# An order of its own for each down stage of a fused mLSTM + GELU kernel

## The chip, the cores and the metric

The kernel runs on one core of one Trainium2 chip. The metric is device microseconds of one execution. The engines are TensorE (PE, with its weight loads shown apart as PEld), VectorE (DVE), ScalarE (ACT), GpSimd (POOL) and SyncE (SP, whose queue issues nearly all DMAs). Each engine works through its own instructions in the order in which the kernel writes them.

## The reference

An mLSTM cell over 4 batches, 8 heads, 768 time steps and head size 40, and a two-layer network with exact GELU (320 to 2048 to 320) on its 3072 output rows. All is float32.

```python
for t in range(S):
    m_new = np.maximum(f_gate[:, :, t] + m, i_gate[:, :, t])
    f_stab = np.exp(f_gate[:, :, t] + m - m_new); i_stab = np.exp(i_gate[:, :, t] - m_new); m = m_new
    C = f_stab[:, :, None, None] * C + i_stab[:, :, None, None] * np.einsum('bhd,bhe->bhde', vt, kt)
    n = f_stab[:, :, None] * n + i_stab[:, :, None] * kt
    denom = np.maximum(np.abs(np.einsum('bhd,bhd->bh', n, qt)[:, :, None]), 1.0)
    y[:, :, t] = 1 / (1 + np.exp(-o_gate[:, :, t])) * np.einsum('bhde,bhe->bhd', C, qt) / denom
x = y.transpose(0, 2, 1, 3).reshape(B * S, H * D)
h = x @ w_in
out = (0.5 * h * (1.0 + erf(h / sqrt(2)))) @ w_out
```

## The kernel before

The sequence is cut into six chunks of 128 steps (c = 0 to 5). Within a chunk the cell is computed as an attention block (scores, weighted by exps of the gates) plus a part from the state carried over from earlier chunks. A chunk's 512 rows then go through the network: an *up* stage (x @ w_in, GELU into the tile `g`) and a *down* stage (g @ w_out). While chunk c is in its down stage, the cell of chunk c+1 is computed in the gaps, so that its rows are ready for the next up stage.

The first chunk and the second's cell follow the order FRONT; the last chunk has a code of its own. Each of the four down stages between (c = 1 to 4, the second to the fifth chunk) follows the order DOWN, a string of steps which `play` carries out one after the other. A word is a letter and, for a step of the cell, the batch (0 to 3). Since every engine keeps the order of the program, the string sets each engine's queue. The letters, with the engine and line of their work:

| word | step | work |
|---|---|---|
| M | mask | POOL L449, on the tile W of gate sums; batch 3's lies in a part of `g` |
| W | weights | ACT L475, 8 exps, in place in W |
| G | gate | ACT L481, sigmoid of the output gate, in `ob` |
| K, Q | transposes of k and q | DVE L497 into kT, qT (two buffers each); Q2 also issues POOL's `vw` (L534) |
| D3 | `vw` of batch 3 | POOL L534 |
| L3 | load of batch 3's k and q | POOL two memsets L487, SP four loads L171 |
| B3 | load of batch 3's gate sums into `g` | SP L188 |
| S0, S2 | scores of two batches | PE L563 (64x64 tiles), DVE L569: times W, four multiplies for each batch |
| C0, C2 | reads of the state, two batches | PE L618 into two banks pf |
| h0, h2 | state update, two batches | PE L629 into the same banks; POOL L642 state times decay; DVE L638 far and L644 state add |
| V | values | PE L665 (128x32 tiles), DVE L673 add; V0 also issues loads of k and v of batch 3 (SP L153) |
| Y | finish | ACT L680 Abs into `den` (one buffer), POOL L681 max and L682 multiply, DVE L686, L687; for batch 0 then ACT L694, a copy to `y_rest` |
| X | transpose of y | PE L705 into px (two banks), ACT L694 copy to `y_rest` for the next batch, L715 x_hi |
| R | split of x | DVE L728 x_lo, L729 x_all; frees px |
| F | half a product, 8 matmuls | PE L1073 |
| N | late sums | DVE L1099, two operations on `g`; what they write is read by F11 and F12 |
| Z | part of a weight sum, in the second chunk only | DVE L783 |
| j | loads for the next cell | SP L171 and L163, up to 20 DMAs |

The down product is made of seven products over halves (a Strassen-like scheme), each in two halves: F1 to F14, one for each F in the string. F1, F2, F5 and F6 accumulate in one PSUM bank, F3 and F4 in a second, F7, F8, F11 and F12 in a third, F9, F10, F13 and F14 in a fourth; two banks stand for the four, and a new one takes the bank that came free first: F7 that of F3 and F4, F9 that of F1 to F6. What follows a product on another engine is written directly behind it:

```python
todo = ((A(0, 0), Bm[0][0], 0, True, p1), (Sm(g.s2), T[2], 1, True, p6),
        (A(1, 0), Bm[1][0], 0, False, p2), (Sm(g.s1), T[1], 2, True, p5),
        (A(0, 1), T[3], 3, True, p7), (A(1, 0), Bm[1][1], 2, False, p3),
        (A(1, 1), T[4], 3, False, p4))
```

p1 (behind F2, L1088) and p2 (behind F6, L1094) are copies on ACT; p6, p5, p7, p3 and p4 (behind F4, F8, F10, F12 and F14, L1084) are adds on DVE, the last two with the sends of the output. F5 has to wait for p1, since it adds into the bank that p1 reads; F11 for p5, F13 for p7.

Exp, Sigmoid and Gelu lie in different function tables of ACT; each change shows as an ACT_TABLE_LOAD.

Of the kernel before, what the change touches and what calls it, by code (L numbers as in the profile page):

```python
# [25 lines left out]


FRONT = """
    I2 O0 g0 L0 P0 L1 E k1 t0 P1 P2 w0 k7 N k2 w1 O1 K L2 Q s0 O3 w2 q D
    k2 d P3 t1 w3 c0 L3 J v0 t2 K K y0 s1 I7 v1 I8 O2 J g1 L4 I5 c1 K I1  # L30
    I2 y1 s2 x0 t3 B4 O4 B5 g2 J x1 s3 v2 c2 L5 y2 H T0 x2 G0 v3 g3 c3 K y3
    M1 J L6 J A x3 M0 K W0 O7 K A O6 O5 J M2 W1 S0 C0 K J J T1 U U
    K L7 V0 K T2 r J J A G2 K G1 Y0 W2 S1 K M3 C1 A J S2 J K W3 K
    V1 C2 Y1 T3 J J U U S3 V2 K K J G3 J Y2 C3 X0 K V3 J K F J F
    K K B8 F J K F F J K F F F R0 X1 J J K F J F K X2 F J
    K F J Y3 K F R1 e J F Z B9 B10 F X3 R2 Z R3 F p"""
DOWN = """
    M0 F Z F L3 W0 M1 Z W1 S0 C0 F F h0 Q2 F K2 G1 D3 B3 Z V0 G2 M2 W2 M3 W3 V1 K3 Q3 F G0 S2 Z Y0 G3 C2 h2 F
    F Y1 X0 V2 V3 F N F j R0 Y2 Y3 X1 F F X2 R1 F R2 X3 R3 F"""


@with_exitstack
def kernel(
# [18 lines left out]
    B, H, S, D = q.shape  # L62
    L = P
    NCH = S // L
# [79 lines left out]
    def load(n, first=0, end=4):  # L144

        if n >= NCH * B:
            return
        c, b = divmod(n, B)
        for src, dst in ((q, qb), (k, kb), (v, vb), (o_gate, None))[first:end]:
            if dst and swapped(c, b):  # L150
                x, to = src[b, :, c * L:(c + 1) * L, :].rearrange("h p d -> p h d"), dst[turn_of(n)][:, :, 0:D]
                for i in range(2):
                    nc.sync.dma_start(out=to[halves[i]], in_=x[halves[1 - i]])  # L153
                continue
            nc.sync.dma_start(out=dst[turn_of(n)][:, :, 0:D] if dst else out_of(n),  # L155
                              in_=src[b, :, c * L:(c + 1) * L, :].rearrange("h p d -> p h d"))
# [136 lines left out]
    def decays_turned(e0, e1, g0, g1):  # L293
        e, g = slice(e0, e1), slice(g0, g1)
        gates_turned((ew[:, e], ewT[:, e]), (gg[:, g], gT[:, g]))

    def decays_last(g0, g1):
        g = slice(g0, g1)
        pd = ps_tr.tile([P, g1 - g0, BH], F32, name="pd", tag="tr")
        nc.tensor.matmul(pd.rearrange("p c n -> p (c n)"), last, gT[:, g].rearrange("p c n -> p (c n)"),  # L300
                         start=True, stop=True)
        by_half = pd.rearrange("p c (n two) -> p c n two", two=2)
        for hip in range(2):
            nc.vector.tensor_copy(out=dec[halves[hip], g], in_=by_half[halves[hip], :, :, hip])
# [65 lines left out]
    def conv_one(i):  # L370

        if i < len(pieces):
            n = bits[i].shape[1]
            lo, hi = bits[i][:, :, 0], bits[i][:, :, 1]
            s = sig[i] = raw.tile([P, WP], F32, name="sig", tag="sig")[:, 0:n]
            p = pow2[i] = raw.tile([P, WP], F32, name="pow", tag="pow")[:, 0:n]
            su, pu = s.bitcast(U32), p.bitcast(U32)

            nc.vector.tensor_scalar(out=pu, in0=hi, scalar1=20, scalar2=0x7FF,  # L379
                                    op0=OP.logical_shift_right, op1=OP.bitwise_and)  # L380
            nc.scalar.activation(out=p, in_=pu, func=AF.Relu, scale=-I23, bias=e_hi)  # L381
            nc.scalar.activation(out=pu, in_=p, func=AF.Relu, scale=-1.0, bias=e_lo)

            nc.vector.tensor_scalar(out=su, in0=hi, scalar1=0xFFFFF, scalar2=0x100000,
                                    op0=OP.bitwise_and, op1=OP.bitwise_or)
            nc.vector.scalar_tensor_tensor(out=s, in0=lo, scalar=2.0 ** -32, in1=su, op0=OP.mult, op1=OP.add)

    def conv_two(i):

        if i < len(pieces):  # L390
            hi, p = bits.pop(i)[:, :, 1], pow2.pop(i)
            pu = p.bitcast(U32)
            nc.vector.scalar_tensor_tensor(out=pu, in0=hi, scalar=0x80000000, in1=pu,
                                           op0=OP.bitwise_and, op1=OP.bitwise_or)
            dst, s = pieces[i][1], sig.pop(i)
            nc.vector.scalar_tensor_tensor(out=dst, in0=s, scalar=2.0 ** -20, in1=p, op0=OP.mult, op1=OP.mult)  # L396
            fetch(i + NB)
# [430 lines left out]
    def first_up_steps(h):  # L828

        def step(k):  # L830
            ups.append((len(ups) + len(tags_next) % 2, (2 * k, 2 * k + 2, HT * h, HT * h + HT)))
            if len(ups) == 2:
                first_up()

        return [lambda k=k: step(k) for k in range(HF // 2)]

    def first_up():
        if len(ups) == 1:
            tags_next.append(1)
        if ups:  # L840
            up_step(first_g, ups)
        ups.clear()
# [201 lines left out]
    def first_down_steps(g):  # L1044
        po = []

        def row(f):

            if f == 0:
                po.extend(ps_mm.tile([P, DM], F32, name="po", tag="ab"[b // 2]) for b in range(B))  # L1050
            for b in range(B):
                nc.tensor.matmul(po[b], g.t[:, f, b * L:(b + 1) * L], w_out[:, f, :], start=(f == 0),  # L1052
                                 stop=(f == NF - 1))
                if f == NF - 1:
                    if b % 2 == 0:
                        o_sb = outp.tile([P, 2, DM], F32, name="o_sb", tag="o_sb")
                    nc.scalar.copy(out=o_sb[:, b % 2, :], in_=po[b])
                    send(0, b, o_sb[:, b % 2, :])

        return [lambda f=f: row(f) for f in range(NF)]  # L1060
# [64 lines left out]
    def play(order, steps):  # L1125

        for word in order.split():
            if word[0] not in "AU":
                first_up()
            steps[word[0]](*[int(x) for x in word[1:].split(",") if x])  # L1130

    def in_turn(steps):
        todo = list(steps)
        return lambda: todo.pop(0)() if todo else None

    def cell_steps(c, letters, before=None):
        cell = Cell(c)
        cell.before = before
        return dict(zip(letters, (cell.mask, cell.weights, cell.gate, cell.turn, cell.scores, cell.carry, cell.values,
                                  cell.finish, cell.turn_y, cell.split_x, cell.load_last, cell.turn_k,  # L1140
                                  cell.turn_q, cell.weigh_last, cell.read_two,
                                  cell.last_M, cell.scores_two, cell.load_next, cell.update_two)))

    def first_blocks():

        copy_chunk(2, range(1))
        for r in (32, 96):
# [5 lines left out]
    steps = dict(P=fetch, L=lambda n: load(n, 0, 2), O=lambda n: load(n, 2, 4), B=load_M, E=second_gates, N=later_gates,  # L1153
                 I=keep_clock, k=warm, D=lambda: decays_turned(0, 2, 0, 1), Q=lambda: decays_turned(2, NCH - 1, 1, NCH - 1),
                 d=lambda: decays_last(0, 1), q=lambda: decays_last(1, NCH - 1), r=halves_out, p=halves_back,
                 A=in_turn(first_up_steps(0)), U=in_turn(first_up_steps(1)), e=first_blocks, F=in_turn(first_down_steps(first_g)),
                 K=in_turn(lambda i=i: conv_one(i) for i in n_pieces), H=products_begin,
                 J=in_turn(lambda i=i: conv_two(i) for i in n_pieces), Z=split_weight)
    steps |= cell_steps(0, "mwgtscvyx") | cell_steps(1, "MWGTSCVYXR")
    play(FRONT, steps)  # L1160
    for c in range(1, NCH):
        if c + 1 == NCH:
            down = LastDown()
            up(None, [], [], down)
            down.products()
            break
        g, later = Hidden(True), []
        steps = cell_steps(c + 1, "MWGTscVYXRLKQDCBSjh", g)
        up(g, weight_sum(1) + weight_sum(2) + weight_sum(3) if c == 1 else [], [lambda b=b: (steps["K"](b), steps["Q"](b)) for b in range(2)])
        if c == 1:  # L1170
            later = weight_sum(4)
        products, late = down_steps(c, g)
        steps |= dict(F=in_turn(products), Z=in_turn(later), N=late)
        play(DOWN, steps)


# [28 lines left out]
```

## Time and profile before

| | us |
|---|---|
| time, median of 3 runs (lowest, highest) | 463.55 (462.91, 463.84) |
| profiled execution, its own time | 463.01 |
| its span, first to last instruction | 461.1 |
| up stages of c = 1 to 4, each | 26.49 |
| down stage of c = 1: 154.99 to 198.70 | 43.71 |
| down stage of c = 2: 225.19 to 268.38 | 43.19 |
| down stage of c = 3: 294.87 to 337.58 | 42.71 |
| down stage of c = 4: 364.07 to 404.82 | 40.75 |
| up and down of c = 5: 404.82 to 461.10 | 56.28 |

Stages are cut where the chain of waits passes from up to down products. In a timeline a row is a group of like instructions with its start, its length, the count, and in brackets the idle time of the engine before it with what ended that. The fifth chunk's down stage (c = 4) is shorter because the last cell updates no state: h0 and h2 have no matmuls there.

### The profile page before, as it was taken

What the parts mean: (1) busy time and instruction counts of PE and PEld (TensorE: products, weight loads), DVE (VectorE), ACT (ScalarE), POOL (GpSimd) and SP (SyncE); (2) the same over time, 40 slices, a digit from 0 to 9 for tenths busy, and PEclk for the clock granted to TensorE, in tenths of its full rate; (3) what the DMA queues carried; (4) which work ended last, traced back from release to release, by engine and by line L of the source; (5) the groups of instructions that cost most, each with busy time, mean ns of one, the idle gap of its engine ahead of it and who ended that gap; (6) DMA issues with size and microseconds to landing.
All of it is one profiled execution on the core that took longest, in us unless ns stands there. A gap on an engine that the chain in (4) does not pass through costs nothing.

```text
span 461.1 us, 13165 instructions
## 1 busy us (share of the span) xinstructions
PE 453.0 (98%) x5432; PEld 402.1 (87%) x5432; DVE 337.8 (73%) x740; ACT 247.3 (54%) x541; POOL 77.9 (17%) x117
## 2 busy tenths in 40 slices
PE   8999999999999999999999999999999999999996
PEld 8787888877788898998899998899998899988996
DVE  8899879798868988754578754578654577699950
ACT  6986999854454594113494113395113395157701
POOL 3002020000010342300542200542300422100000
PEclk9999999999999999999999999999999999999999
DMA  8997993258967655219955219953018950210001
GB/s 153 206 216 190 211 221 97 73 131 226 157 164 157 117 91 97 66 50 181 161 88 95 66 58 179 156 93 46 4 57 170 166 99 13 80 36 2 1 0 58
DMA packets 174876, 51.12 MB, mean 111 GB/s; under 512 B 154752, under 2 KB 168352, under 8 KB 174816
## 3 DMA queue, kind: packets, MB, share of 16 engines
q1 hardware_dynamic: 174496, 49.95, 53.4%
q8 instruction: 43, 0.70, 0.7%
q10 hardware_dynamic: 320, 0.33, 0.2%
q14 instruction: 17, 0.14, 0.1%
HBM read 45.47 MB, written 10.03 MB: 120 GB/s over the span
## 4 chain that ended last, share of the span: by engine, by line
PE 93%; DVE 3%; DMA 2%; SPq 1%; issue 1%; ACT 0%; DVEq 0%
PE po L1073 26%; PE pu L957 23%; PE po L1052 8%; PE pu L814 6%; PE pu L968 6%; PE po L927 6%; PE ph L665 4%; PE ps L563 3%; PE pu L820 2%; PE px L705 2%; PE pf L618 2%; PE ps L547 1%; SPq L155 1%; PE pf L629 1%; PE cold L228 1%; DMA ob<-in_o_gate_dram 1%
## 5 line engine op out<-in xcount | busy, mean ns | idle before, releaser
L1073 PE MATMUL po<-w_out,g 128*128 128x160 f32 x512 | 74.4, 302 | 0.0
L972 ACT ACTIVATE g<-pu 128x512 f32<-128x512 f32 x64 | 32.2, 620 | 77.4 <-PE pu L968 77.4
L1073 PEld LDWEIGHTS po<-w_out,g 128*128 128x128 f32 x512 | 70.1, 190 | 1.9 <-ACT g L972 1.3
L957 PE MATMUL pu<-x_hi,w_in_hi 128*128 128x512 f32 x160 | 39.0, 387 | 0.0
L475 ACT ACTIVATE W<-W,aT 128x128 f32<-128x128 f32 x128 | 38.7, 388 | 0.1
L957 PE MATMUL pu<-x_lo,w_in_lo 128*128 128x512 f32 x160 | 37.8, 379 | 0.0
L449 POOL TENSOR_SCALAR_AFFINE_SELECT W<-W 128x1024 f32<-128x1024 f32 (+2 forms) x20 | 24.1, 1209 | 80.3 <-DMA W<-M_d 70.0
L1073 PE MATMUL po<-w_sums,sums 128*128 128x160 f32 x256 | 36.9, 302 | 0.0
L1073 PEld LDWEIGHTS po<-w_sums,sums 128*128 128x128 f32 x256 | 35.0, 190 | 0.4
L1052 PE MATMUL po<-w_out,g 128*128 128x320 f32 x128 | 35.2, 433 | 0.0
L957 PEld LDWEIGHTS pu<-x_hi,w_in_hi 128*128 128x128 f32 x160 | 29.5, 189 | 5.7 <-ACT g L972 1.3
L957 PEld LDWEIGHTS pu<-x_lo,w_in_lo 128*128 128x128 f32 x160 | 30.2, 189 | 4.3
L1052 PEld LDWEIGHTS po<-w_out,g 128*128 128x128 f32 x128 | 24.0, 190 | 9.6
L534 POOL TENSOR_TENSOR vw<-vb,ewT 128x328 f32<-128x328 f32 x12 | 8.8, 745 | 136.3 <-DMA vb<-in_v_dram 90.7
L569 DVE TENSOR_TENSOR W<-ps,W 128x256 f32<-128x256 f32 (+1 forms) x48 | 18.1, 416 | 17.0 <-PE ps L563 7.1
L957 PE MATMUL pu<-x_all,w_mid 128*128 128x512 f32 x80 | 30.3, 379 | 0.0
L957 PE MATMUL pu<-x_all,w_in_mid 128*128 128x512 f32 x80 | 30.3, 379 | 0.0
L814 PE MATMUL pu<-first_x,w_in 128*128 128x256 f32 x128 | 29.0, 382 | 0.0
L814 PEld LDWEIGHTS pu<-first_x,w_in 128*128 128x128 f32 x128 | 23.8, 190 | 3.4 <-DVE w_in L396 0.3
L801 DVE TENSOR_TENSOR sums<-g 128x512 f32<-128x512 f32 x16 | 12.3, 770 | 19.6 <-ACT g L972 19.6
L773 DVE TENSOR_TENSOR w_in_mid<-w_in_hi,w_in_lo 128x512 fp32r<-128x512 f32 x20 | 13.7, 685 | 16.5 <-PE pu L957 16.5
L381 ACT ACTIVATE pow<-pow,e_hi 128x320 f32<-128x320 uint32 (+1 forms) x26 | 16.1, 620 | 15.2 <-DVE pow L379 15.2
(199 smaller groups left out, 952.1 us busy)
## 6 DMA issues: line engine op xcount, KB each, us to landing
W<-M_d SPq DMA_DIRECT2D x16, 512.0 KB, 5.3
bits<-in_moe_w_in_dram SPq DMA_DIRECT2D x20, 256.0 KB, 4.3
bits<-in_moe_w_out_dram SPq DMA_DIRECT2D x16, 320.0 KB, 3.2
blocks<-kq_d SPq DMA_DIRECT2D x32, 128.0 KB, 3.2
ob<-in_o_gate_dram SPq DMA_DIRECT2D x24, 160.0 KB, 4.5
out_dram<-o_sb SPq DMA_DIRECT2D x36, 80.0 KB, 2.0
kq_d<-in_k_dram SPq DMA_DIRECT2D x32, 80.0 KB, 2.5
kq_d<-in_q_dram SPq DMA_DIRECT2D x32, 80.0 KB, 2.4
```

The source lines that it names most:

```text
L381: nc.scalar.activation(out=p, in_=pu, func=AF.Relu, scale=-I23, bias=e_hi)
L449: nc.gpsimd.affine_select(out=x, in_=x, compare_op=OP.is_ge, fill=1.0e30, base=base, pattern=[[0, H], [1, x.shape[2]]], channel_multiplier=-1)
L475: nc.scalar.activation(out=W[n][:, h, :], in_=src, func=AF.Exp, scale=-1.0, bias=aT[:, self.c, r:r + 1])
L569: nc.vector.tensor_tensor(out=w[r, :, t], in0=ps[i][hip][r, :, t], in1=w[r, :, t], op=OP.mult)
L665: nc.tensor.matmul(ph[r, h, :], Pm[:, h, r], vb[turn_of(n)][:, h, :], start=True, stop=True)
L814: nc.tensor.matmul(banks[-1][e][:, i - i0, :], in_tile(i, x)[:, e, i % 2 * P:(i % 2 + 1) * P], first_x[:, x, t0:t1], start=(x == 0 and i = ...
L927: nc.tensor.matmul(in_pairs(po[t]), x[:, t * L:(t + 1) * L], in_turns(w), start=(f, k) == first, stop=(f, k) == last, skip_group_check=True)
L957: nc.tensor.matmul(in_pairs(pus[i][e]), w[k][:, e, i * P:(i + 1) * P], in_turns(x[:, k, :]), start=(n == 0 and k == 0), stop=False, skip_g ...
L968: nc.tensor.matmul(in_pairs(pu[e]), w[r, i // 2, i % 2 * P:(i % 2 + 1) * P], in_turns(x[r, NX, :]), start=False, stop=(n == 2), skip_group ...
L972: nc.scalar.activation(out=g.t[:, HF * e + i, :], in_=pu[e], func=AF.Gelu, scale=4097.0)
L1052: nc.tensor.matmul(po[b], g.t[:, f, b * L:(b + 1) * L], w_out[:, f, :], start=(f == 0), stop=(f == NF - 1))
L1073: nc.tensor.matmul(bank[k][:, t, :], lhs(j, t), rhs(j), start=(first and t == 0 and j == 0), stop=(t == 1 and j == HF - 1), skip_group_che ...
```

## The change

DOWN is replaced by three orders: DOWN1 for c = 1, DOWN2 for c = 2 and 3, DOWN3 for c = 4. They have the words of DOWN in another order. FRONT is only broken into lines differently.

```diff
-DOWN = """
-    M0 F Z F L3 W0 M1 Z W1 S0 C0 F F h0 Q2 F K2 G1 D3 B3 Z V0 G2 M2 W2 M3 W3 V1 K3 Q3 F G0 S2 Z Y0 G3 C2 h2 F
-    F Y1 X0 V2 V3 F N F j R0 Y2 Y3 X1 F F X2 R1 F R2 X3 R3 F"""
+DOWN1 = """
+    M0 F W0 G1 K2 M1 W1 M2 L3 G2 Q2 F B3 S0 C0 h0 Z K3 D3 F F G0 V0 F Q3 V1 W2 M3 W3 j F Y0 F Y1 S2 C2 G3 h2 F
+    X0 R0 F V2 N Z V3 Y2 Z X1 Z Y3 F F X2 R1 F R2 F X3 R3 F"""
+DOWN2 = """
+    M0 K2 M1 W0 W1 G1 F S0 C0 h0 M2 G2 Q2 G0 F F L3 B3 K3 D3 Z Q3 F M3 V0 V1 Y0 W2 j F F W3 S2 C2 Z h2 F Y1 F
+    F X0 N Z G3 V2 V3 R0 F Y2 Y3 F Z X1 F X2 R1 R2 F X3 F R3"""
+DOWN3 = """
+    G1 F M0 M1 W0 W1 K2 S0 C0 h0 M2 D3 G2 F F F Q2 B3 L3 M3 V0 K3 G0 V1 F W2 j F Q3 W3 S2 Z C2 h2 Y0 Z Y1 F F
+    X0 F N G3 V2 V3 F R0 Y2 Z X1 Y3 F F Z X2 R1 R2 F X3 F R3"""
...
-        play(DOWN, steps)
+        play(DOWN1 if c == 1 else DOWN2 if c < NCH - 2 else DOWN3, steps)
```

In all three, the first state update (h0) stands directly behind S0 and C0; DOWN has F3 and F4 between. L3 stands behind M1 and M2 (in DOWN ahead of both), K2 ahead of S0. The exps and sigmoids run W0 W1 G1 G2 W2 W3 G0 G3 in DOWN, W0 G1 W1 G2 G0 W2 W3 G3 in DOWN1, W0 W1 G1 G2 G0 W2 W3 G3 in DOWN2 and G1 W0 W1 G2 G0 W2 W3 G3 in DOWN3. In DOWN2 Y0 stands ahead of W2, in DOWN1 Y0 and Y1 ahead of S2, and in DOWN2 and DOWN3 R3 stands behind F14.

## The prediction

> **What bounds the kernel now.** I read the page first, then busy time by stage, then the chain of waits and the timeline of each down stage. The page:
>
> ```profile
> PE 453.0 (98%) x5432; PEld 402.1 (87%) x5432; DVE 337.8 (73%) x740; ACT 247.3 (54%) x541; POOL 77.9 (17%) x117
> PE 93%; DVE 3%; DMA 2%; SPq 1%; issue 1%; ACT 0%; DVEq 0%
> ```
>
> TensorE is the bound nearly everywhere, so an order can gain only what PE loses between its instructions. Busy time in the four down stages (window, its length, PE, PEld, DVE, ACT, POOL):
>
> ```profile
> 154.99:198.70 43.71, 42.87 (x813) 41.27 (x814) 35.74 (x84) 23.78 (x60) 15.90 (x22) 1.00 0.47 88
> 225.19:268.38 43.19, 42.88 (x814) 41.30 (x814) 31.67 (x68) 23.78 (x60) 15.02 (x22) 1.00 0.50 91
> 294.87:337.58 42.71, 42.66 (x814) 41.17 (x814) 30.70 (x68) 23.79 (x60) 16.29 (x21) 1.00 0.37 58
> 364.07:404.82 40.75, 40.65 (x751) 39.57 (x750) 29.46 (x60) 24.15 (x61) 12.67 (x15) 1.00 0.37 70
> ```
>
> Idle PE is 0.84 in the second chunk, 0.31 in the third, 0.05 and 0.10 in the last two. The second chunk's loss is at S2, where the timeline of PE shows
>
> ```profile
> 174.39 1.44 PE L563 MATMUL ps<-qT,kT 64*64 64x128 f32 x56 [0.55 <-DVE qT L497]
> 177.38 0.73 PE L629 MATMUL pf<-vw,kb 128*40 128x41 f32 x27 [0.29 <-issue]
> ```
>
> DVE is late with K3 and Q3. The chain of waits shows the same in the third chunk, and its absence in the fifth, as the length of S2; and what a product costs behind other work:
>
> ```profile
> 243.78 1.72 PE ps L563 x44
> ...
> 381.72 1.50 PE ps L563 x64
> ...
> 390.60 4.54 PE po L1073 x32
> 395.14 0.33 PE px L705 x3
> 395.47 4.35 PE po L1073 x32
> ```
>
> A pair of products behind a V (128x32 tiles) takes 4.54, behind an X (128x128) 4.35: each return from small tiles costs 0.19. ACT in the second chunk's stage, where every change between Exp and Sigmoid has a table load:
>
> ```profile
> 159.62 0.43 ACT L1088 COPY o_sb<-po 128x320 f32<-128x320 f32 x1 [2.51 <-issue]
> 160.06 1.28 ACT L475 ACT_TABLE_LOAD   x1
> 161.36 4.78 ACT L475 ACTIVATE W<-W,aT 128x128 f32<-128x128 f32 x16
> 166.15 1.28 ACT L481 ACT_TABLE_LOAD   x1
> 167.45 0.83 ACT L481 ACTIVATE ob<-ob 128x320 f32<-128x320 f32 x2
> ```
>
> **The change, by stage.** FRONT has the same words. Each new order has the same 61 words as DOWN, so nothing is added but table loads. Below, t runs from the stage's first product; durations are the rows' (W 2.45, G 0.47, S 1.50, C 0.92, h 0.74, V 0.75, X 0.33, F 2.18).
>
> *Second chunk, DOWN1.* ACT ends the gelus at t=2.2. The order W0 G1 W1 G2 F2 .. G0 W2 W3 .. F6 needs five loads ahead of F6's copy, DOWN's W0 W1 G1 G2 W2 W3 three. F2's copy is done at 2.2 + 4 loads 5.2 + two W 4.9 + two G 0.9 + 0.4 = 13.6; F6's at 13.6 + G0 0.5 + load 1.3 + W2, W3 4.9 + 0.4 = 20.7 (19.8 before). PE, h0 now behind C0: F1, F2 4.54, S0 1.50, C0 0.92, h0 0.74, F3, F4 4.54, V0 0.77 gives 13.0 when F5 comes, which adds into the bank that F2's copy still reads: it waits 0.65. S2 comes at 21.4, when K3 and Q3 (DVE, 18.2) are done: the 0.84 is gone. The tail is worse. Y0 and Y1 now stand before S2's multiplies on DVE, and Y0's Abs (ACT) behind W3 and F6's copy, at 20.9. A Y is Abs 0.20, POOL 0.23 and 0.81, DVE 0.49 in a row with gaps, about 1.9, and Y1 waits for `den` (one buffer): they end at 22.6 and 24.8, and DVE, done with V1's add at 18.7, has nothing else meanwhile. DOWN starts those multiplies at 21.2 (176.07). From 24.8 DVE has no gap: S2's multiplies 3.1, h2 2.3, F8's add 0.5, R0 1.0, V2's add 0.5, N 2.85, Z 0.5, V3's add 0.5, Y2 0.75 gives 36.7, and ACT's copy to y_rest 37.05; PE, from S2 at 21.4 by the rows of S2, C2, h2, F8, X0, F9, V2, V3, X1, F10 and F11, is at X2 at 35.9 and waits 1.1. Then Z, Z 1.05, Y3 1.7 and F10's add 0.45 give 39.95; F13 adds into the bank which that add reads. F13, X3 and F14 end at 39.95+2.18+0.33+2.18 = 44.7: **+1.0**.
>
> *Third and fourth, DOWN2.* ACT keeps the grouping (W0 W1 G1 G2 G0, then W2 W3, G3: four loads as before), and M1 no longer stands behind L3's memsets on POOL, so W0 starts at 2.2 and not behind F2's copy. h0 behind C0 makes four groups of small tiles instead of five, 0.19 each stage; S2 (at 18.2) finds Q3 done at 14.7, 0.22 each. PE alone would end at 41.9 from the rows, and DOWN's own rows add up to 42.48 where the fourth chunk measures 42.71, so 42.1 is the floor. But Y0 stands before W2, and its copy to y_rest (ACT) ends with a chain: L3's two memsets (0.94 each) now stand on POOL behind the two state multiplies, M2 and vw and end at 9.5; three of L3's four loads and B3 wait behind them on SP, as do V0's kb and vb (landing near 16 and 18, wanted at 20.7 and 29: hidden); B3 issues at 10.3 and lands 4.6 later (the page's median for g<-M_d), M3 1.8 to 17.0, then Y0's max, multiply and DVE's share to 18.6, copy 18.9. W2: load and exps to 22.65; F6's copy 0.4; W3 to 25.5. DVE: S2's multiplies end 27.15, h2 29.4, Y1 30.15, add 30.6, N 33.4, adds 34.3, R0 35.3, add 35.75, Y2 36.55, Y3 38.55, add 39.0, R1 40.0. F11 meets N's halves within 0.1. X2 waits 0.1 for y_rest (37.1), X3 0.4 for R1, which frees its bank; X3 and F14 end at 42.55. That is **-0.65** for the third and **-0.15** for the fourth. R3 now stands behind F14's add (0.49): the next up stage wants x_lo 1.73 (8 matmuls of 0.216) after F14 and has it after about 1.2; without that cover 0.5 each.
>
> *Fifth, DOWN3.* One more load (G1 first), but F2's copy is done at 12.2 for F5 at 13.0, S2 meets Q3 with 1.1 to spare, X3 meets R1 with 0.6. No state is updated, so DOWN has four groups already. **0**, bounds -0.1 to +0.5.
>
> j's 20 loads and copies issue as soon as Q2 frees `blocks`, as now (172.44), and only sends stand behind them. The state update behind its reads frees nothing else: its POOL half waits only for C0's reads already.
>
> What no row shows is a bank or DVE handing over in these orders; I bound the second chunk by F5's wait alone (+0.65-0.84 = -0.2) and by the late copy shifting the whole tail (+2.0), third and fourth by the floor (-1.1, -0.6) and by +1.1 each. I take the walked values, whose links are nearly all rows of this trace. Sum: 1.0-0.65-0.15+0 = +0.2 on an execution of 463.01 (span 461.1, 1.9 around it), 0.54 below the median of 463.55; so 463.8.
>
> On the loads the Trainium skill speaks against the change ("ScalarE: Activation LUTs", What ACT_TABLE_LOAD costs): about 2.66 for a switch, of which 1.38 is a drain. The trace disagrees: the load at 160.06 lasts 1.28 and the exps start at 161.36. By the page F2's copy would come 5.5 later and F6's 6.9, and an estimate of the sum from its figure is +7.1 instead of +0.2.
>
> **The rivals.**
> 1. *Only PE's savings come*, the tails being hidden: the second chunk loses its 0.84, third and fourth reach 42.1 (-1.1, -0.6): 463.55-2.5 = 461.0, or 462.3 if half of it comes. For: PE is 98% busy and ACT 54%. Against: F5 and the DVE tail above are sums of rows. 0.18.
> 2. *Y0's copy holds up W2 in DOWN2.* R1 at 40.0 already stands 0.4 behind PE, so from M3's end at 17.0 on every further us is one at the stage's end. For: in the fifth chunk M3 came 5.15 after B3's issue (371.45 to 376.60), not 4.6, and loads of `blocks` took up to 6.0 where 3.4 is the median. Against: half of the delay would overlap. At 1.1 in each of two stages: 463.8+2.2 = 466.0. 0.30.
> 3. *Single activations between two loads don't hide the switch*, as the rows of 16 and 8 exps may: each of the five switches ahead of F6's copy then costs as much as two loads, 1.28 more, and the second chunk 6.4 more than the forecast: 470.2. Against: at 166.15 and 168.28 only two sigmoids stand between loads, and nothing is idle. 0.02. The page named above has this rule.
> 4. *The order does nothing*, since K2 still waits for S0's reads of kT (two buffers) and DVE takes the rest as before: 463.55. Against: M1, W0 and h0 do move. Within the forecast.
>
> **How the numbers follow.** A measurement of this kernel tells about 0.2% (0.93) from no change. The forecast, second chunk paying what the third and fourth win, has 0.50, with its own range 462.7 to 464.9; it is mostly "same", with 0.02 below and 0.06 above. Rival 1 gives faster 0.18, rival 2 and 3 slower 0.32. Faster 0.20, same 0.42, slower 0.38. The range takes in more than half of rival 1 (to 462.0; 0.07 is below) and two thirds of rival 2 (to 466.8, where the two stages lose 1.5 each; 0.10 of it and rival 3 are above).
>
> **What would show it.** The second chunk's stage at 44.7, ACT with six table loads ahead of its last gelu load, F5 idle some 0.6 behind ACT's copy at L1088, X2 behind y_rest; PE never waiting for qT. The third's and fourth's both near 42.5, idle before X3 for DVE's x_all, POOL's M3 ahead of Y0. Fifth unchanged. I am wrong if the second chunk's falls below 43.7, if the middle ones stay above 43.2, or if an up stage leaves 26.49.

## The result and the profile after

| | before | after |
|---|---|---|
| time, median | 463.52 us (6 runs) | 465.53 us (6 runs) |
| profiled execution, and its span | 463.01, 461.1 | 464.30, 462.3 |
| down stage c = 1 | 43.71 | 44.44 |
| c = 2 | 43.19 | 42.62 |
| c = 3 | 42.71 | 42.94 |
| c = 4 | 40.75 | 41.40 |

The ratio of the times is 1.0041, 95% interval 1.0027 to 1.0055: the changed kernel is slower by 0.4%. The profiled execution of after was the fastest of its six: by the medians the change costs 2.0 us, and its profile shows 1.2 of them. The four stages together lose 1.04 of the 1.2 us by which the spans differ. The up stages measure 26.49 or 26.50 as before.

Busy time of each engine over the span, and the chain that ended last by engine, from the page of after:

```profile
PE 451.2 (98%) x5432; PEld 400.3 (87%) x5432; DVE 332.9 (72%) x740; ACT 252.0 (55%) x544; POOL 74.4 (16%) x117
PE 73%; DVE 9%; ACT 7%; DMA 4%; SPq 3%; issue 2%; POOL 2%; DVEq 0%; ACTq 0%; POOLq 0%
```

TensorE is busy for 1.8 us *less* than before and the execution is longer all the same. Of the 1.8, 1.1 lie in the first 10 us (PE busy for 7.61 instead of 8.70), ahead of every changed stage, and 0.69 in the four stages. There the orders do remove work between small tiles, and more than that comes back as idle time of PE. The chain's share of other engines rises from 7% to 27%. By stage (window, length, busy PE, PEld, DVE, ACT, POOL):

```profile
155.06:199.50 44.44, 42.91 (x813) 40.88 (x814) 34.05 (x84) 26.59 (x62) 13.22 (x19) 1.00 0.46 87
225.99:268.61 42.62, 42.40 (x815) 41.07 (x814) 28.83 (x66) 23.89 (x60) 13.13 (x20) 1.00 0.50 88
295.10:338.04 42.94, 42.33 (x814) 40.96 (x814) 28.43 (x66) 23.89 (x60) 12.46 (x19) 1.00 0.35 56
364.53:405.93 41.40, 40.73 (x749) 39.62 (x750) 25.72 (x58) 25.67 (x62) 7.57 (x12) 1.00 0.34 66
```

PE busy is 0.48 and 0.33 less in the two middle stages and 0.08 more in the fifth chunk's; PE idle is 1.53, 0.22, 0.61 and 0.67 where it was 0.84, 0.31, 0.05 and 0.10. The timeline of PE names each gap (start, length, group, and in brackets the idle time before it):

```profile
168.61 2.44 PE L1076 MATMUL po<-w_out,g 128*128 128x160 f32 x16 [0.57 <-ACT o_sb L1091]
191.23 0.41 PE L708 MATMUL px<-ident,ob 128*128 128x128 f32 x2 [0.44 <-DVE ob L690]
194.56 2.44 PE L1076 MATMUL po<-t,g 128*128 128x160 f32 x16 [0.52 <-DVE o_sb L1087]
...
265.92 0.41 PE L708 MATMUL px<-ident,ob 128*128 128x128 f32 x2 [0.17 <-DVE x_all L732]
...
316.44 0.19 PE L621 MATMUL pf<-state,qT 64*64 64x41 f32 x1 [0.55 <-issue]
...
378.23 0.27 PE L668 MATMUL ph<-vb,W 128*32 128x41 f32 x3 [0.61 <-issue]
```

The first three are F5 behind ScalarE's copy of p1, X2 behind a Y, and F13 behind p7's add, all in the second chunk. The fourth is X3 behind R1. The last two are of another kind: the last matmul of C2, and the last three of the 128 of V0 and V1, start late with nothing that they wait for; "issue" means that the profile shows no cause. V1's inputs were long there: DVE's last multiply for it ended at 376.10. These two gaps are what the prediction has no step for.

### The profile page after: what moved, and what is told of

It is laid out like the page before. It is cut to its first block, busy times and chain, and to the rows that moved or that the text cites. A ratio compares the mean times of both kernels' runs of the same rounds, so it can differ in the third digit from the quotient of the medians.

```text
span 462.3 us, 13146 instructions
## 1 busy us (share of the span) xinstructions
PE 451.2 (98%) x5432; PEld 400.3 (87%) x5432; DVE 332.9 (72%) x740; ACT 252.0 (55%) x544; POOL 74.4 (16%) x117
## 4 chain that ended last, share of the span: by engine, by line
PE 73%; DVE 9%; ACT 7%; DMA 4%; SPq 3%; issue 2%; POOL 2%; DVEq 0%; ACTq 0%; POOLq 0%
PE pu L960 23%; PE po L1076 14%; PE po L1055 7%; PE pu L817 6%; PE po L930 6%; PE pu L971 5%; DMA blocks<-kq_d 3%; PE ph L668 3%; ACT W L478 2%; PE pu L823 2%; SPq L174 1%; PE ps L550 1%; PE px L708 1%; PE ps L566 1%; SPq L158 1%
## 5 line engine op out<-in xcount | busy, mean ns | idle before, releaser
L452 POOL TENSOR_SCALAR_AFFINE_SELECT W<-W 128x1024 f32<-128x1024 f32 (+2 forms) x20 | 21.3, 1073 | 82.5 <-DMA W<-M_d 61.6
L697 ACT COPY y_rest<-ob 128x128 f32<-128x128 f32 x16 | 4.7, 296 | 41.7 <-DVE ob L690 35.3
L804 DVE TENSOR_TENSOR sums<-g 128x512 f32<-128x512 f32 x16 | 11.0, 688 | 18.7 <-ACT g L975 18.7
```

The lines of the kernel that those rows point to most:

```text
L452: nc.gpsimd.affine_select(out=x, in_=x, compare_op=OP.is_ge, fill=1.0e30, base=base, pattern=[[0, H], [1, x.shape[2]]], channel_multiplier=-1)
```

## The experiments

Two theories. **A**: TensorE ran out of program. **B**: it waits for data or a buffer that the profile does not name. What A rests on: the page lists the queue that brings programs,

```profile
q8 instruction: 42, 0.69, 0.7%
```

that is pieces of 16 KB each, nearly all TensorE's (5432 weight loads and 5432 matmuls are 42.4 times 256). The trace has the times of these reads. One read ran from 375.70 to 376.93, and the DMA view of 375.6 to 377.0 shows it beside 1435 small packets of the kernel's own loads:

```profile
q1 hardware_dynamic: 1435, 0.12, 75.0%
q8 instruction: 1, 0.02, 5.5%
```

1.30 us after its end V1 went on. Counting all TensorE instructions that the trace records (weight loads, matmuls, semaphore waits), every gap named issue stands within one instruction of place 192 of 256: a border between pieces. The Trainium skill ("Runtime: NRT & Kernel Launch", Instruction fetch mechanics) states that the program comes in blocks of 256 instructions and the next is fetched while the current one runs. It calls the cost of crossing mostly hidden; that is where it and these traces part.

The table gives all kernels that ran. Stages run here from the record of the first down matmul to that of the first up matmul, 0.2 shorter than above; "issue" is the sum of PE's gaps of that name over 0.14 us from c = 1's down stage to c = 4's. Ratios are to the kernel before on the same chip.

| kernel | time | ratio (interval) | c=1 | c=2 | c=3 | c=4 | issue |
|---|---|---|---|---|---|---|---|
| before | 463.23 to 463.69 | 1 | 43.51 | 42.99 | 42.51 | 40.55 | 0.55 |
| after | 465.53 | 1.0041 (1.0027, 1.0055) | 44.24 | 42.42 | 42.73 | 41.20 | 1.16 |
| again (the change) | 465.35 | 1.0036 (1.0023, 1.0048) | 44.22 | 43.08 | 42.35 | 41.49 | 0.88 |
| only1 | 464.66 | 1.0021 (1.0010, 1.0031) | 44.23 | 43.60 | 42.80 | 40.44 | 0.84 |
| only2 | 463.55 | 1.0000 (0.9988, 1.0012) | 43.11 | 42.58 | 44.09 | 40.45 | 1.71 |
| only3 | 464.61 | 1.0015 (1.0006, 1.0023) | 43.66 | 42.73 | 43.10 | 41.34 | 0.62 |
| shift12 | 463.53 | 1.0006 (0.9997, 1.0016) | 44.23 | 42.12 | 43.03 | 40.41 | 0.50 |
| shift44 | 466.78 | 1.0062 (1.0048, 1.0077) | 44.24 | 44.53 | 42.68 | 40.34 | 2.46 |
| bshift40 | 465.10 | 1.0041 (1.0024, 1.0057) | 42.99 | 44.27 | 42.51 | 40.45 | 1.43 |
| bshift76 | 465.82 | 1.0051 (1.0034, 1.0068) | 44.20 | 42.71 | 43.25 | 41.86 | 2.73 |
| group | 463.93 | 1.0009 (0.9996, 1.0023) | 42.73 | 42.88 | 42.87 | 41.73 | 1.77 |
| f5first | 464.56 | 1.0024 (1.0013, 1.0035) | 44.22 | 42.44 | 43.27 | 41.12 | 1.10 |
| only1g | 462.95 | 0.9986 (0.9976, 0.9996) | 42.73 | 43.23 | 43.17 | 40.48 | 0.77 |
| best8 | 462.32 | 0.9977 (0.9965, 0.9988) | 42.64 | 43.23 | 42.81 | 40.33 | 0.50 |

### One order at a time: only1, only2, only3, again

```diff
+        play(DOWN1 if c == 1 else DOWN, steps)          # only1
+        play(DOWN2 if c in (2, 3) else DOWN, steps)     # only2
+        play(DOWN3 if c == 4 else DOWN, steps)          # only3
```

only1: 

> DOWN1 in the second chunk alone, DOWN in the other three. Theory A (the walk by queues): the second chunk's down stage is 44.4 us as in the profile of the change (43.7 before), the others as before; the kernel loses about 0.7 us, ratio 1.0015. Theory B (PE runs dry of instructions: the 0.55 and 0.61 us gaps named issue in the fourth and fifth chunk come from the denser small-tile work): no such gap above 0.3 us outside the second chunk, and the loss is again 0.7. Theory C (the part of the 2.0 us loss that the profiled execution doesn't show, 1.2 us, belongs to the second chunk): the loss is near 2 us.

only2: 

> DOWN2 in the third and fourth chunk alone. Theory A: the third chunk's stage 42.6 (43.2 before), the fourth's 42.4 without a gap named issue (42.7 before): the kernel gains 0.5 to 0.9 us, ratio 0.998 to 0.999. Theory B: the gaps come with the denser small-tile groups, 0.3 to 0.6 us in each stage: the fourth's is 42.9, and the kernel gains 0.3 or nothing. Theory C2 (the unseen 1.2 us belongs to DOWN2, by loads that land late in front of K2, K3 or M3): the kernel loses 0.5 us or more.

only3: 

> DOWN3 in the fifth chunk alone. Theory A: no change (40.75), ratio 1.000. Theory B: one gap named issue of 0.6 us in this stage, as in the change: a loss of 0.6 us, ratio 1.0014. Theory C3 (the unseen 1.2 us belongs here): a loss of 1.5 us or more.

again: 

> The change as it is, on the same chip, for a second profile of it. Theory A: the three parts add up to it, within 0.5 us; the stages are again 44.4, 42.6, 42.4 to 42.9 and 40.8 to 41.4. Theory B: gaps named issue again, 0.5 us or more in all over the before, at the same instructions. Theory C: a stage that is over 0.5 us longer than in the first profile holds the unseen 1.2 us.

The parts add up: +0.21%, 0.00% and +0.15% are 0.36%, again measures 0.36%. By time, then, the loss comes with DOWN1 and DOWN3, each known to some 0.1%. But a part is more than its own stage, since an order also moves what stands behind it: of only1's 0.97 us the second chunk's stage holds 0.72, and the third, still in DOWN, has a gap named issue of 0.84 in V3 where before has 0.26, which no theory for only1 allowed. DOWN1's 44.2 with its three waits is the same in each profile that has it with G1 in its old place. DOWN2 gained nothing by time (expected 0.5 to 0.9 by A, 0.3 or nothing by B). It brings its gain and loses it elsewhere: 42.58 in the third chunk, and 44.09 in the fourth, with the largest gap of all, at the same place as in after. From only2's timeline of PE:

```profile
317.08 0.25 PE L625 MATMUL pf<-state,qT 64*64 64x41 f32 x2 [1.71 <-issue]
```

DOWN3's stage is 0.65, 0.79 and 0.94 longer than before's in after, only3 and again, in the first and the last by the gap in V1 (0.61, 0.88). In only3 the border lies 3 matmuls earlier and the read of the next piece begins at 374.24 instead of 375.70; V1 runs through, so the 0.6 us that B expected came without B's gap: a second weakness takes the place: K3's load lands late, and S2 takes 2.25 instead of 1.39. From only3's timeline of DVE:

```profile
381.47 0.71 DVE L504 STREAM_TRANSPOSE kT<-blocks 128x512 f32<-128x512 f32 x1 [2.78 <-DMA blocks<-kq_d]
```

again has two stages outside what was expected of it. The fifth, with its gap of 0.88, is one; the third, 43.08, is 0.66 longer than after's, with no gap named issue. By its theory C a part of the loss that after's profile does not show belongs there. What makes the third chunk's stage long or short is shown with the account of the prediction.

### Moving the borders: shift12, shift44

Dummy matmuls stand at the start of the kernel, where TensorE has nothing else to do. A few small ones more and a large one less move all later borders without touching the orders of the stages.

```diff
-    fill(42)
-    warm(6)
+    fill(49)    # shift44: 67
+    warm(5)     # shift44: 3
```

shift12: 

> The kernel after, with seven more of the small dummy matmuls that start the kernel and one less of the large ones: 12 TensorE matmuls more in the program, no longer at the start, nothing else changed. Theory A: TensorE's program is fetched in pieces of 256 instructions (16 KB, 43 fetches in a profile); a new piece is asked for when one is begun, so one whose matmuls take under some 3 us leaves TensorE idle under the name issue. In the profiles so far the instruction behind each such gap stands at place 192 or 193 of 256 (counting all recorded TensorE instructions). Then 12 more matmuls ahead move every border 12 matmuls back, and the piece that ends in V1 of the fifth chunk takes in 10 more slow down matmuls (some 1.4 us): the gaps behind C2 of the fourth chunk (0.55) and in V1 of the fifth (0.6 to 0.9) vanish, stages 42.2 to 42.5 and 40.4 to 40.6 instead of 42.73 and 41.20, time 0.8 to 1.4 us under the kernel after. Theory B: the gaps are a wait for data that the profile doesn't name (v loads, PSUM buffers): dummy matmuls at the start change nothing, time as after within 0.3 us, the fifth chunk again 41.2 to 41.5.

shift44: 

> The same with 25 more small dummy matmuls and three large ones less: 44 TensorE matmuls more in the program. Theory A (pieces of 256 instructions): now five pieces of the down stages hold nearly nothing but small-tile matmuls and take 1.6 to 2.4 us; new gaps named issue appear at new places, in the second to fifth chunk, in sum some 4.8 us against 1.4 us by the same sum for the kernel after: time 2.5 to 6 us over the kernel after. Theory B (data): as after within 0.3 us.

shift12 takes both gaps away. Its fourth and fifth chunk:

```profile
294.64:337.67 43.03, 42.39 (x815) 40.99 (x813) 28.16 (x66) 23.97 (x60) 12.45 (x20) 1.00 0.36 58
364.36:404.77 40.41, 40.36 (x750) 39.38 (x749) 25.67 (x58) 25.47 (x62) 7.64 (x12) 1.00 0.36 68
```

In the fifth chunk PE is idle for 0.05 and the stage is 0.8 shorter, with not one word of DOWN3 changed. By the ratios shift12 is 1.4 to 1.6 us under the two measurements of the change, more than the 0.8 to 1.4 expected. Its fourth chunk is longer than expected: a new gap of 0.50 opened there, in the products ahead of S2 and at a border again. Theory B, by which dummies 300 us earlier change nothing, is out. shift44 goes the other way, by 1.0 to 1.2 us where I expected 2.5 to 6: right in sign, too large in size. The waits of PE in its trace from 150 to 406 us (engine, line, releaser: us in total, times, longest):

```profile
PE pf L632 <- issue: 2.0, 2, 1.1
PE po L1076 <- ACT o_sb L1091: 0.6, 1, 0.6
...
PE ph L668 <- issue: 0.5, 1, 0.5
```

Three new gaps in h and V, and none where after has its two. Of the 2.7 us by which shift44's span exceeds after's, 1.5 lie ahead of the second chunk's down stage, 0.77 of them one more such gap at a border, in V at 94.16.

The matmuls between the two borders around V1 of the fifth chunk show a part of why. F has 16 matmuls in the record in 2.18 us (two for each of its 8), V0 and V1 have 128 in 1.60:

| kernel | F | V | gap |
|---|---|---|---|
| before | 20 | 106 | none |
| after, again | 2 | 125 | 0.61, 0.88 |
| group | 2 | 125 | 1.14 |
| only3 | 5 | 122 | none |
| shift12 | 14 | 113 | none |
| best8 | 10 | 117 | none |
| f5first | 17 | 109 | none |
| bshift76 | 18 | 105 | 1.21 |

In DOWN the piece takes in 20 slow matmuls; DOWN3 has one F less ahead of V0, so the border moves 16 matmuls into V1, and what is left is run through in 1.8 us. The count of long matmuls does not decide alone: bshift76, below, has 18 and a gap all the same.

### The kernel before shifted: bshift40, bshift76

```diff
-    fill(42)
-    warm(6)
+    fill(65)    # bshift76: 84
+    warm(3)     # bshift76: 2
```

bshift40: 

> The kernel before, with 23 more small dummy matmuls at the start and three large ones less: 40 matmuls more. Theory A: its own gaps (0.29 at h2 of the second chunk, 0.26 at V3 of the third) go, smaller ones may come elsewhere; by the same sum 0.6 instead of 1.3 us, so 0.3 to 0.9 us under the kernel before. Theory B: as before within 0.3 us.

bshift76: 

> The kernel before with 76 more matmuls at the start (42 small dummies more, four large less). By the refined sum of theory A (request ten matmuls ahead, 4.1 us) the kernel before loses 2.4 us to gaps where 0.55 us were seen, with 40 more 3.5 us, with 76 more 1.6 us: so the sum is too large by a factor, and only its sign is trusted. Expected: 0 to 0.8 us under the kernel before; the 0.55 wait for qT in the second chunk stays. If it comes out over 0.5 us slower, the sum can't rank layouts that differ by under 1 us, and only gaps seen in a trace may be acted on.

Both wrong in sign: 1.9 and 2.4 us slower. bshift40's two old gaps went as expected, and one of 1.43 came at h2 of the third chunk. The places are those of A, the sizes are not what my sum gave. bshift76's waits of PE in the same window:

```profile
PE ph L665 <- issue: 2.7, 3, 1.2
PE ps L563 <- DVE qT L497: 0.5, 1, 0.5
```

I had counted V's pieces as long enough one by one. The piece before the gap at 392.83 lasts 4.0 us, and the two ahead of it are as short (4.1 and 4.0). Their reads begin 0.6 to 0.7 us into the piece, the one that the gap waits for 2.9 (390.27). What delays it is not shown. A sum over single pieces can't rank layouts that differ by 1 us.

### G1 behind W1: group

```diff
-    M0 F W0 G1 K2 M1 W1 M2 L3 G2 Q2 F ...
+    M0 F W0 K2 M1 W1 G1 M2 L3 G2 Q2 F ...
```

group: 

> The kernel after with G1 moved behind W1 in the second chunk's order: ScalarE's function tables change places twice less ahead of F2's copy (two loads of 1.28 us less). Theory (the steps of the prediction, confirmed in size by the second chunk's 44.24 in three profiles): the copy of p1 comes 2.5 us earlier, F5 waits for nothing, the chain behind it (o_gate, y, the add) comes earlier and the waits of 0.44 and 0.52 at the stage's end go too: second chunk 42.6 to 43.0, time 1.0 to 1.6 us under the kernel after. Rival: the waits at the end come from the vector engine's own queue (S2 C2 work ahead of Y2): only F5's 0.57 goes, stage 43.7, time 0.4 to 0.6 us under.

As expected: 1.3 to 1.5 us under the change, the second chunk's stage 1.5 shorter:

```profile
155.13:197.86 42.73, 42.29 (x815) 40.74 (x813) 34.64 (x85) 24.10 (x60) 13.06 (x19) 1.00 0.47 91
```

ScalarE's timeline has two loads ahead of p1's copy where after has four (the first of each is at 157.33 and 157.19):

```profile
158.63 4.79 ACT L478 ACTIVATE W<-W,aT 128x128 f32<-128x128 f32 x16
163.43 1.28 ACT L484 ACT_TABLE_LOAD   x1
164.72 0.83 ACT L484 ACTIVATE ob<-ob 128x320 f32<-128x320 f32 x2
165.46 0.40 ACT L1091 COPY o_sb<-po 128x320 f32<-128x320 f32 x1
```

The copy comes 2.83 earlier, counted from the stage's start, F5 and X2 wait for nothing, and F13's 0.52 becomes 0.37. So the tail's waits were for the most part ScalarE's table loads, handed on. group keeps the gaps in C2 (0.63) and V1 (1.14).

### F5 ahead of V0: f5first

```diff
-    ... M2 D3 G2 F F F Q2 B3 L3 M3 V0 K3 G0 V1 F W2 j F ...
+    ... M2 D3 G2 F F F F Q2 B3 L3 M3 V0 K3 G0 V1 W2 j F ...
```

f5first: 

> The kernel after with one F (16 matmuls, 2.2 us) of the fifth chunk put ahead of V0 instead of behind V1; no dummies, same places of the borders outside. Theory A: the piece that held V0 and V1 alone now holds 2.2 us of slow matmuls as well, so its successor is there in time: no gap in V1, fifth chunk 40.4 to 40.6 instead of 41.2 to 41.5, time 0.6 to 1.0 us under the kernel after; the gap behind C2 of the fourth chunk stays. Rival: the order itself of V0 V1 ahead of their surroundings costs the time (a wait on the vector engine or on the loads of the next group, as the 0.86 us at S2 in only3's profile); the gap only moves, fifth chunk 41.0 to 41.5, time as after within 0.3 us.

The gap in V1 is gone, as A has it. But the stage is 41.12, not 40.5: F5 comes 2.2 earlier and meets p1's copy, so it waits 0.63. From its timeline of PE:

```profile
377.13 2.44 PE L1076 MATMUL po<-w_out,g 128*128 128x160 f32 x16 [0.63 <-ACT o_sb L1091]
379.50 1.56 PE L668 MATMUL ph<-vb,W 128*32 128x41 f32 x128
```

The time, 0.6 to 0.8 us under the change, is near what I expected, for a reason that this stage does not give: it is only 0.1 to 0.4 shorter. That part I leave open.

### Both cures, and the second chunk alone: best8, only1g

best8 has group's order and `fill(47)`, `warm(5)` (8 matmuls more); only1g is only1 with G1 behind W1.

best8: 

> Both cures at once: the kernel after with G1 behind W1 in the second chunk's order (as group) and with 8 more matmuls at the start (five small dummies more, one large less). Theory A says that the request for a piece goes out about ten matmuls ahead of its border where TensorE is busy and at the border where small tiles run through, and that the piece is usable some 4.1 us later; summed over the matmul times of the group kernel that leaves 1.1 us of gaps without the shift, 0.1 with 8 matmuls and 0.6 with 12. Expected: second chunk 42.7 as in group, no gap behind C2 of the fourth chunk or in V1 of the fifth (40.4 to 40.6), time 462.0 to 463.0, that is 0.9 to 1.9 us under group and 0.5 to 1.4 us under the kernel before. Rival: the two gains don't add, since the shorter second chunk moves the transfers against each other; time as group or as the kernel before, 463.4 to 464.0.

only1g: 

> The kernel before with the new order in the second chunk alone (as only1), G1 behind W1 in it, no dummies: how much of best8's 0.9 us under the kernel before is the second chunk's order, and how much the orders of the third to fifth chunk. If the second chunk is all of it: stages 42.7, 42.9 to 43.6 (the gap in V3 of the third chunk, 0.3 to 0.8, as in only1, since its border lies where only1's does), 42.5 to 42.8, 40.4; time 1.4 to 1.7 us under only1's 464.66, that is 462.7 to 463.3, and best8's remaining 0.4 to 1.0 us under it come from the borders of the pieces. If the later chunks' orders are worth something beyond their gaps: over 463.3.

Both times came out inside their ranges; of the stages, only1g's fourth (43.17, expected 42.5 to 42.8, with a gap of 0.30 behind C2) did not. best8 is 0.23% faster than the kernel before and 0.6% faster than the change. Its four stages:

```profile
155.03:197.67 42.64, 42.23 (x814) 40.74 (x813) 34.93 (x85) 24.08 (x60) 13.07 (x19) 1.00 0.48 91
224.37:267.60 43.23, 42.38 (x815) 40.79 (x813) 28.84 (x66) 23.97 (x60) 13.32 (x21) 1.00 0.50 88
294.29:337.10 42.81, 42.26 (x814) 40.89 (x813) 28.42 (x66) 24.05 (x60) 12.43 (x19) 1.00 0.36 57
363.80:404.13 40.33, 40.28 (x750) 39.29 (x749) 25.75 (x58) 25.46 (x62) 7.63 (x12) 1.00 0.36 70
```

The second and the fifth carry the gain (0.87 and 0.22 under before); the third and the fourth are 0.24 and 0.30 over it. Two gaps named issue are left in the fourth (0.17 and 0.33, where the sum allowed 0.1). only1g shows that the second chunk's order, once its loads are grouped, is most of it: 0.14% faster than before with DOWN everywhere else. best8 and only1g were compared with other runs of the kernel before, and their intervals overlap, so whether DOWN2 and DOWN3 with good borders are worth anything is not settled.

## Why the prediction was right or wrong

It gave 463.8 in 462.0 to 466.8, most likely no change. The time, 465.5, is in the range and slower by 0.4%, which had 0.38.

**Second chunk, +1.0: right in mechanism, a little large.** It measured +0.73. All four links are in the trace: six table loads; p1's copy ending at t = 13.6, as walked, with F5 waiting 0.57 for it (0.65 walked); S2 no longer waiting for qT; F13 waiting 0.52 for p7's add (0.4). X2's wait was sized wrong: 0.44 instead of 1.1, and for DVE's `ob`, not for the copy to y_rest, so DVE's chain of sums ran some 0.7 ahead of my walk. That alone is more than the 0.3 by which the term is too large, and group shows that the cause named, the loads ahead of p1's copy, is the one.

**Third and fourth, -0.65 and -0.15: the third right in mechanism and partly by luck in size, the fourth not.** The third measured -0.57, ending on X3 behind R1 (0.17; 0.4 walked). M3 ended at t = 17.4 and the copy of y_rest at 19.4, 0.4 and 0.5 behind the walk, and the chain behind M3 was 0.3 shorter than walked, so two errors nearly cancel. Also, 0.26 of before's third stage was its gap in V3, for which the walk had no term. The walk is right that the stage hangs on M3. In the seven profiles that have DOWN2 and no gap named issue in this stage, t being counted from the first down matmul:

| kernel | M3 ends at t | stage |
|---|---|---|
| shift12 | 17.12 | 42.12 |
| after | 17.43 | 42.42 |
| f5first | 17.47 | 42.44 |
| only2 | 17.60 | 42.58 |
| group | 17.89 | 42.88 |
| again | 18.10 | 43.08 |
| best8 | 18.24 | 43.23 |

The stage ends 25.0 us after M3 in each. M3 waits for B3's load: it starts 4.9 to 6.1 us after B3's issue, where the walk had the load land after 4.6. M3 in after and in best8, and what follows in best8 (F11 behind N, X3 behind R1):

```profile
241.54 1.81 POOL L452 TENSOR_SCALAR_AFFINE_SELECT g<-g 64x1024 f32<-64x1024 f32 x2 [5.11 <-ACT den L683]
...
240.81 1.81 POOL L452 TENSOR_SCALAR_AFFINE_SELECT g<-g 64x1024 f32<-64x1024 f32 x2 [5.94 <-DMA g<-M_d]
257.39 2.49 PE L1076 MATMUL po<-w_out,g 128*128 128x160 f32 x16 [0.50 <-DVE g L1102]
265.17 0.41 PE L708 MATMUL px<-ident,ob 128*128 128x128 f32 x2 [0.29 <-DVE x_all L732]
```

In after ACT's Abs, named there, had long been done; B3's load landed 0.15 before M3 started. The fourth stage measured +0.23: the gap of 0.55 behind C2. S2's wait is gone as walked, and S2 and C2 now run through in one piece of the program that holds 2.6 us of matmuls; before's piece there took 3.1 and showed no gap. The old order is not far from one: in only3 and only1g, which have DOWN in the fourth chunk, the same border cost 0.19 and 0.30.

**Fifth, 0: the step that failed.** It measured +0.65. The copy, S2 and X3 did what the walk had; V1 did not run in the length of its rows. I took matmul groups at their durations in the trace of before wherever they stood, and put no term for TensorE's own program. By the stages the sum should have been +1.0 instead of +0.2; the two gaps named issue are 1.16, and nothing in the sum stood for them. The other 0.8 of the 2.0 us lies in executions without a profile and is not explained; a larger gap (0.88 in again) or a later M3 would add to it.

The hint was in the trace of before. One of the two lines shown for its second chunk has 0.29 idle "<-issue" in the middle of h2, and I gave it no cause. It was a border too.

**The rivals.** Rival 2's time, 466.0, is close to what came, and in after that is luck: M3 was late by 0.4 there, and the third chunk still gained. But its mechanism is real in the third chunk, where each us that M3 is late is one at the stage's end, and not half of one. In again and best8, 1.1 and 1.2 behind the walk, it took the whole gain of that stage (43.08 and 43.23 against before's 42.99). The fourth does not follow M3: without their gaps its stages are 42.2 to 42.5, with M3 ending at 17.0 to 18.3. Rival 1 failed on F5 and the tail, as argued against it. Rival 3 is out: the loads last 1.28 each, with the next activation straight behind, and the copy came when the walk said. By the Trainium skill ("ScalarE: Activation LUTs", What ACT_TABLE_LOAD costs) it would have come 5.5 later; this trace disagrees. Rival 4 is out as well: the second chunk's stage is 0.7 longer in each of the six profiles that have DOWN1 as it is.

## What to carry to other kernels

An idle engine with "issue" as the reason is a finding and not noise: look where the program's pieces end, by counting the engine's instructions, and when their reads landed. Small matmuls can be run faster than their instructions can be brought, so keep some long matmuls in each stretch of 128. Around V1 of the fifth chunk, 2 of them gave a gap in each of three profiles and 5 to 20 gave none in five, but 18 gave one in bshift76: they help only as far as the read comes in time. A new order, or even a few instructions more at the start of the kernel, moves all later borders and can shift the time (here by 0.3% down and 0.5% up); before an order is judged by less than that, measure it at two or three shifts.

Group activations by their function table ahead of anything that TensorE waits for: here one gate moved behind one group of exps was worth 1.5 us.

## What the runs showed of the hardware

- In the 14 profiles PE has 24 gaps over 0.14 us named issue between 150 and 406 us. Each ends 1.20 to 1.58 us after the end of a read of 16 KB of program, and each stands within one instruction of place 192 of 256.
- The next read begins 1.11 to 2.18 us after the gap. A read itself lasts 0.88 to 2.26 (median 1.04). Two reads never begin less than 3.3 us apart; 128 matmuls of V take 1.60.
- The same border can cost much or little. With S2 and C2 of the fourth chunk at the same border, after, only2, group and f5first lost 0.55, 1.71, 0.63 and 1.10, and again 0.12. What makes a read late is not settled; each profile shows one execution.
- Filling TensorE's program with 12 dummy matmuls at the start made the changed kernel 0.3% faster, with 44 0.2 to 0.3% slower.
